# Attention and feed-forward in one kernel: a cosine with one sine, four pooled score products per late pair, and another way of setting the order of instructions

## The chip, the cores and the metric

The kernel runs on one core of a Trainium2 chip. The metric is the device time of one execution in microseconds. The engines are TensorE (PE in the rows; PEld is its weight load), VectorE (DVE), ScalarE (ACT), GpSimd (POOL) and SyncE (SP), which issues most of the transfers. TensorE's clock has two levels, 1.2 and 2.4 GHz, and the rows give the granted clock as a share of full speed.

## What is computed

The reference, cut to what matters:

```python
batch, n_heads, seq, head_dim = (8, 8, 576, 64)
q_d = q.reshape(B, H, Sd, 4, D).mean(axis=3)      # k_d, v_d alike, Sd = 144
out_d = sm_attn(q_d, k_d, v_d)                    # softmax attention over 144 pooled positions
out_up = np.repeat(out_d, 4, axis=2)
mask = np.abs(pos[:, None] - pos[None, :]) < 4    # local attention of 7 neighbours
out_local = np.matmul(softmax(np.where(mask, scale * q @ k.T, -1e9)), v)
x = (out_up + out_local)                          # as (4608, 512)
h = x @ w_in                                      # (4608, 2048)
g = h * np.cos(h)
return g @ w_out                                  # (4608, 512)
```

All tensors are fp32 (the weights arrive as pairs of 32-bit words). The kernel makes up for 16-bit products by splitting each factor into a high and a low fp16 part.

## The kernel before, in words

**Work.** Two heads make a pair, so there are 8 x 4 = 32 pairs. A pair goes through five steps: `u_qk` loads q and k and pools them (sum over 4 positions), `u_v` loads v, `u_s` makes local and pooled scores and their softmax, `u_t` transposes the probabilities, `u_pv` multiplies by v and writes the result, as high and low part, into one of four tiles of x (384 tokens each, 12 of them in all). Batches 0 and 1 (`NEARLY` = 2) go through early forms of these steps, batch 1 in two parts (`part_s`, `part_t`, `part_pv`). The other six batches, 24 pairs, are the late pairs, whose scores are made in `late_s`: 48 local products and 16 pooled ones, the latter with 32 columns of weights each (line 912), both fp32, each shown as two instructions in the trace.

**Feed-forward.** For each of 12 token tiles and 16 chunks of 128 hidden features, `gemm1` (line 1410) makes h, `cosine` makes g = h cos(h) as high and low fp16, and `gemm2` (line 1430) adds to three output banks. From tile 4 on, `Quad` (line 1335) makes h of two chunks by a scheme with fewer products. There are 192 calls of `cosine`, each on 128 x 384 values. It works by lines 1386 to 1393: ACT adds a large constant so that the sum rounds to whole turns, DVE subtracts it and h, ACT takes the sine of half the angle and the square, DVE makes h (sin^2 - 1/2), ACT rounds to fp16 (gh), POOL or DVE takes the rest (gl, line 530).

**Weights.** `w_load` and `w_split` bring and split each weight chunk (lines 575 to 590), `sum_w`, `sum_x` prepare sums for `Quad`, and `square`, `range_w` and `judge` watch that the 16-bit form is allowed.

**Order.** Nothing is issued in the order of the code. Each operation is entered into a `Plan` with its engine (or a choice of engines), a duration, what it reads and writes, the mean use that TensorE makes of its time (`util`) and its number of TensorE instructions (`num`). `run` places operations by a key, engine by engine, `schedule` improves the keys by running forwards and backwards, then tries the changes in `PICKS` (random additions to keys in a window of time) and keeps each that shortens the planned time. `run` holds a model of stops for TensorE's instructions (`FETCH`). The figures that the planner has for a pair of batch 0 are: local scores 1.30 us at a share of 0.25, pooled scores 0.65 at 0.42, two transposing products of 0.29 at 0.31, pooled values 2.10 at 0.51, local values 1.52 at 0.16.

**Unread products.** TensorE's clock falls when it has little to do. When the order stands, the code at the end walks through it and puts products of an identity that nobody reads (`wide`, line 1600, 128x512) into idle stretches of TensorE, spread behind the operations that it waits for, and more of them where its share over a trailing stretch would fall below `share` = 0.42 (`again` = 0.72 for a while after a planned stop), for operations planned before `watch` = 115 us.

**Stores.** `gemm2` copies each finished bank (line 1448) and SP stores it (line 1454); the last three copies end the program.

## Time and profile before

| | |
|---|---|
| runs | 914.15, 909.73, 913.79 us; median 913.79 |
| profiled execution | span 910.3 us from first to last instruction; no other time is given for it |
| TensorE busy | 889.4 us (98%), mean granted clock 0.994 |
| DVE, ACT, POOL busy | 711.2, 693.1, 486.2 us |
| instructions | 28740 |
| moved by DMA | 103.96 MB |

Busy TensorE includes the unread products. Products overlap in the pipeline, so a group of them is read from its start to the start of the next group, as the chain of waits does, and not from the mean duration. The chain is the work that ended last, followed back from the last instruction. Idle time of an engine other than the one that bounds a stage costs nothing.

### The profile page before, as it was taken

How to read it: one execution, taken by the hardware profiler on the slowest of the kernel's cores; microseconds unless marked ns; L12 is line 12 of the kernel's file. 1: busy time of each engine (PE TensorE's matmuls, PEld its weight loads, DVE VectorE, ACT ScalarE, POOL GpSimd, SP SyncE). 2: the span in 40 equal slices, each digit the busy share in tenths (PEclk: the TensorE clock that was granted, in tenths of full speed). 3: DMA queues.
4: the chain of work that ended last, by engine and by line, in shares of the span. 5: the costliest groups of instructions: out<-in, count | busy, mean ns of one | idle time of the engine just before them, and what ended most of it. 6: DMA issues, size and time to landing. Idle time of an engine off the chain costs nothing.

```text
span 910.3 us, 28740 instructions
## 1 busy us (share of the span) xinstructions
PE 889.4 (98%) x11673; PEld 579.9 (64%) x11673; DVE 711.2 (78%) x1514; ACT 693.1 (76%) x1542; POOL 486.2 (53%) x601
## 2 busy tenths in 40 slices
PE   8999999999999999999999999999999999999996
PEld 4665665555555555677767677666776777777773
DVE  6479788888889998877689887986689867846772
ACT  3458898888678876886887886986888987776764
POOL 4288753537768875644356543653468734522221
PEclk9899999999999999999999999999999999999998
DMA  7864176205453743232433443344344431124501
GB/s 245 255 223 142 37 276 214 83 1 95 113 131 80 169 99 99 63 94 67 119 88 101 121 114 96 89 111 125 102 135 119 112 105 38 56 96 140 174 2 39
DMA packets 100863, 103.96 MB, mean 114 GB/s; under 512 B 47280, under 2 KB 73648, under 8 KB 100720
## 3 DMA queue, kind: packets, MB, share of 16 engines
q1 hardware_dynamic: 99424, 99.67, 37.5%
q0 software_dynamic: 1296, 2.36, 1.8%
q8 instruction: 93, 1.52, 0.7%
q14 instruction: 50, 0.41, 0.1%
HBM read 81.05 MB, written 16.22 MB: 107 GB/s over the span
## 4 chain that ended last, share of the span: by engine, by line
PE 83%; DVE 7%; ACT 5%; DMA 2%; issue 2%; POOL 1%; SPq 0%; DVEq 0%; POOLq 0%; ACTq 0%
PE bank L1430 36%; PE bank L1335 22%; PE bank L1410 11%; PE bank L1600 3%; PE bank L906 2%; PE bank L1203 1%; PE bank L1184 1%; PE bank L912 1%; DMA q<-qT 1%; PE bank L1179 1%; DVE prob L932 1%; PE bank L1196 1%; PE bank L858 1%; ACT L946 1%; ACT L1389 1%
## 5 line engine op out<-in xcount | busy, mean ns | idle before, releaser
L1335 PEld LDWEIGHTS <-wdi 128*128 128x128 f16 x2400 | 203.8, 98 | 59.7 <-issue 3.8
L1430 PE MATMUL bank<-wdo,gh 128*128 128x512 f16 x696 | 207.1, 379 | 0.0
L1335 PE MATMUL bank<-wdo,wdi 128*128 128x192 f16 x1344 | 141.7, 246 | 0.8 <-DVE wdi L1356 0.3
L1430 PE MATMUL bank<-wdo,gl 128*128 128x512 f16 x348 | 131.7, 379 | 0.0
L1410 PEld LDWEIGHTS <-wdi 128*128 128x128 f16 x768 | 74.3, 98 | 56.3 <-issue 2.4
L530 POOL TENSOR_TENSOR gl<-tr,gh 128x384 f16<-128x384 f32 x60 | 59.2, 987 | 69.3 <-ACT gh L1393 51.0
L1430 PEld LDWEIGHTS <-gh 128*128 128x128 f16 x696 | 63.9, 98 | 41.4 <-issue 1.5
L1430 PE MATMUL bank<-wdo,wdi 128*128 128x512 f16 x342 | 86.9, 379 | 0.5 <-ACT ob L1448 0.5
L1430 PE MATMUL bank<-wdo,wdo 128*128 128x512 f16 x315 | 79.8, 379 | 0.7 <-ACT ob L1448 0.7
L1389 ACT ACTIVATE tr<-tr 128x384 f32<-128x384 f32 x98 | 50.9, 521 | 20.8 <-DVE tr L1387 20.3
L1430 PEld LDWEIGHTS <-gl 128*128 128x128 f16 x348 | 34.0, 98 | 41.1
L1386 ACT ACTIVATE tr<-bank,bmagic 128x384 f32<-128x384 f32 x66 | 37.8, 573 | 19.0 <-PE bank L1410 9.9
L1390 ACT ACTIVATE tr<-tr 128x384 f32<-128x384 f32 x98 | 50.4, 517 | 1.2
L1391 DVE SCALAR_TENSOR_TENSOR tr<-tr,bank 128x384 f32<-128x384 f32 x66 | 36.0, 545 | 18.0 <-ACT tr L1390 17.7
L1430 PEld LDWEIGHTS <-wdo 128*128 128x128 f16 x342 | 32.1, 98 | 28.1 <-issue 1.7
L1430 PEld LDWEIGHTS <-wdi 128*128 128x128 f16 x342 | 32.2, 98 | 27.2 <-issue 1.5
L530 POOL TENSOR_TENSOR gl<-wdo,gh 128x384 f16<-128x384 f32 x28 | 26.2, 937 | 43.3 <-ACT gh L1393 31.5
L1251 DVE TENSOR_TENSOR rec<-rec 128x192 f32<-128x192 f32 (+2 forms) x92 | 47.0, 512 | 0.7
L1351 DVE TENSOR_TENSOR bank<-bank,wdo 128x384 f32<-128x384 f32 x64 | 35.9, 560 | 14.6 <-PE bank L1335 13.8
L956 POOL TENSOR_TENSOR prob<-prob,su 128x432 f32<-128x432 f32 x24 | 24.4, 1018 | 37.9 <-DVE su L953 28.7
L530 POOL TENSOR_TENSOR wdo<-rec,wdo 128x384 f16<-128x384 f32 (+1 forms) x36 | 34.1, 953 | 17.2 <-ACT wdo L1296 11.2
L530 POOL TENSOR_TENSOR gl<-wdi,gh 128x384 f16<-128x384 f32 x28 | 28.3, 1010 | 26.6 <-ACT gh L1393 25.6
(408 smaller groups left out, 2451.8 us busy)
## 6 DMA issues: line engine op xcount, KB each, us to landing
vl<-vl SPq DMA_DIRECT2D x26, 384.0 KB, 3.8
vd<-vdn SPq DMA_DIRECT2D x24, 384.0 KB, 3.9
wdi<-w_in SPq DMA_DIRECT2D x16, 512.0 KB, 6.0
wdo<-w_out SPq DMA_DIRECT2D x16, 512.0 KB, 7.4
again<-w_in SPq DMA_DIRECT2D x32, 256.0 KB, 3.4
again<-w_out SPq DMA_DIRECT2D x32, 256.0 KB, 3.6
q<-qT SPq DMA_DIRECT2D x26, 292.0 KB, 4.0
k<-kT SPq DMA_DIRECT2D x26, 292.0 KB, 3.9
```

The lines of the kernel that those rows point to most:

```text
L530: f = lambda e: lambda: e.tensor_tensor(out=out(), in0=in0(), in1=in1(), op=ALU.subtract)
L956: f = lambda e, get=get, by=by: lambda: e.tensor_tensor(out=get(), in0=get(), in1=by(), op=ALU.mult)
L1251: f = lambda e: lambda: e.tensor_tensor(out=out(), in0=in0(), in1=in1(), op=op)
L1335: pe.matmul(bank.get()[:, half * HT:(half + 1) * HT], w(i, a), x(l, a), start=start and k == 0, stop=k == 5, skip_group_check=not start)
L1351: pl.op("DVE", _dve(TT), lambda: dve.tensor_tensor(out=by.get()[:, :TT], in0=by.get()[:, :TT], in1=s.get(), op=ALU.add), r=[mid, s], w=[by])
L1386: pl.op("ACT", _act(m, banked, 1), lambda: act.activation(tr.get(), h(), AF.Identity, bias=bmagic), r=r, w=[tr])
L1389: pl.op("ACT", _act(m, False), lambda: act.activation(tr.get(), tr.get(), AF.Sin, scale=PI / fm.h), w=[tr], tab="sin")
L1390: pl.op("ACT", _act(m, False), lambda: act.activation(tr.get(), tr.get(), AF.Square, scale=math.sqrt(fm.ratio)), w=[tr])
L1391: pl.op("DVE", _dve(m), lambda: dve.scalar_tensor_tensor(out=tr.get(), in0=tr.get(), scalar=0.5 * fm.ratio, in1=h(), op0=ALU.subtract, op1 ...
L1410: pe.matmul(ph.get()[:, :m], w[:, i, kc, :], x[:, kc, :], start=(n == 0), stop=(n == 3 * KC - 1))
L1430: pe.matmul(o, (gh, gh, gl)[k].get()[:, sl], wo.get()[:, (0, 1, 0)[k]], start=(c == c0 and k == 0), stop=(c == c1 - 1 and k == 2))
L1600: return pe.matmul(s[2].get(), ident_b, ident_b.unsqueeze(1).broadcast_to([P, 4, P]), start=True, stop=True)
```

## The change

Three parts.

**Cosine.** ACT divides h by a turn, adds a quarter and writes int32, so that the conversion rounds to whole turns; DVE multiplies the turns back and subtracts h; ACT takes one sine with a quarter turn as bias, which is the cosine; DVE multiplies by h. The square is gone.

**Pooled scores of late pairs.** Four products with 128 columns of weights take the place of 16 with 32. The sixteen columns of queries that are left over are now read at other partitions, so a subtraction and two small stores use other row groups.

**Order and unread products.** `FETCH` goes from `run`. A new `replay` walks through each planned order, with stops for instructions in blocks of 256, and sets the unread products while it walks; the search takes its total as the score. The share is 0.60 everywhere before 140 us. `PICKS` is a longer list, all of whose entries are applied one after the other, to keys or to the choice of engine. Durations and counts of the planner are adapted. A weight split can be staged in PSUM where `SPLIT` says so, which returns 0. One of the last three stores is issued by ACT.

```diff
-FETCH = (448, 10.6, 256, 17.0, 5.2, 3.6)
+BLOCK, FIRSTS, SEQ, FETCH, CROWD, WARM = 256, 448, 105, 3.8, 1.0, 4.6
...
-CFG = dict(cold=6.8, queue=0.0, alttol=0.9, iters=8, mix=0.0, tabpen=3.2, lat=0.2, latself=0.13, latpe=0.25, late=0.17, port=1.0, lead=5.0, lead0=14,
-           fgap=0.4, f0=0.8, fend=300.0, warm=0, fill=0.8, share=0.42, again=0.72, cool=6.0, watch=115.0)
+CFG = dict(cold=6.8, queue=0.0, alttol=0.9, iters=8, mix=0.0, tabpen=3.2, lat=0.2, latself=0.13, latpe=0.25, late=0.17, port=0.55, lead=5.0, lead0=14,
+           fgap=0.4, f0=0.8, fend=300.0, warm=0, fill=0.85, share=0.6, again=0.72, cool=6.0, watch=140.0)
...
             total, start = self.run(key, False)
-            if best is None or total < best[0]:
-                best = (total, start, key)
+            score = self.replay(start)
+            if best is None or score < best[0]:
+                best = (score, start, key)
...
+        for kind, seed, lo, width, sigma, share in self.picks:
             for o in self.ops:
-                if lo <= best[1][o][0] < lo + width and rnd.random() < share:
-                    key[o] += rnd.gauss(0, sigma)
+                if lo <= best[1][o][0] < lo + width and draw(seed, o.i, 0) < share:
+                    x = sigma * (draw(seed, o.i, 1) + draw(seed, o.i, 2) + draw(seed, o.i, 3) - 1.5)
+                    if kind:
+                        self.lean[o] = self.lean.get(o, 0.0) + x
+                    else:
+                        key[o] += x
...
+    def replay(self, start):
...
+        def burst(t, dur, n, ready):
+            nonlocal used, edge, limit, seq
+            step, left, first = dur / max(1, n), n, used
+            seq = max(seq, ready)
+            if edge < first + n:
+                x = max(seq + (edge - first) * 0.0045, when(edge - SEQ))
+                asked.append(x + FETCH + (CROWD if x > 60.0 and any(a + 1.5 < x < b for a, b in full[-3:]) else 0.0))
+                edge += BLOCK
+            while left:
+                k = min(left, limit - used)
+                if not k:
+                    t, limit = max(t, asked.pop(0)), limit + BLOCK
+                    seq = max(seq, t)
+                    continue
+                t, used, left = t + k * step, used + k, left - k
...
+                    for (x, d), (y, _) in zip(marks, marks[1:] + [(t - 0.2, None)]):
+                        j, stop = 0, x + (y - x) * CFG["fill"]
+                        while max(free["PE"], x) + 0.22 < stop:
+                            wide(x)
+                            j += 1
...
+                    if 4.0 < o.start < CFG["watch"]:
+                        j = 0
+                        while j < 16:
+...
                            wide(0.0)
+                            j += 1
...
+    SPLIT = lambda k, c: 0
...
             for i in range(2):
-                for g in range(4):
-                    for h in range(2):
-                        hs, at = slice(64 * h, 64 * h + 64), SD - BS if i else BS * g
-                        pe.matmul(banks[h].get()[BS * g:BS * (g + 1), i * SD:(i + 1) * SD], qkd.get()[hs, 0, at:at + BS], qkd.get()[hs, 1, :],
-                                  start=True, stop=True)
-        pl.op("PE", 1.55, mm, r=[q, k, qkd], pw=banks, w=loc + poo, slack=SLACK, num=256)
+                for h in range(2):
+                    hs = slice(64 * h, 64 * h + 64)
+                    at = (SD - P + BS * h) * i
+                    few = qkd.get()[hs].rearrange("p a n -> p (a n)")[:, at:at + P]
+                    pe.matmul(banks[h].get()[:, i * SD:(i + 1) * SD], few, qkd.get()[hs, 1, :], start=True, stop=True)
+        pl.op("PE", 1.55, mm, r=[q, k, qkd], pw=banks, w=loc + poo, slack=SLACK, num=209)
...
-        less(1, lambda: smd.get()[BS:2 * BS, 2:3, :SD], slice(1, 2), [wide0], BS, 2 * BS)
+        less(1, lambda: smd.get()[2 * BS:3 * BS, 2:3, :SD], slice(1, 2), [wide0], 2 * BS, 3 * BS)
...
-        pl.op("ACT", _act(m, banked, 1), lambda: act.activation(tr.get(), h(), AF.Identity, bias=bmagic), r=r, w=[tr])
-        pl.op("DVE", _dve(m), lambda: dve.scalar_tensor_tensor(out=tr.get(), in0=tr.get(), scalar=MAGIC * fm.h, in1=h(),
-                                                               op0=ALU.subtract, op1=ALU.subtract), r=r, w=[tr], shares=not banked)
-        pl.op("ACT", _act(m, False), lambda: act.activation(tr.get(), tr.get(), AF.Sin, scale=PI / fm.h), w=[tr], tab="sin")
-        pl.op("ACT", _act(m, False), lambda: act.activation(tr.get(), tr.get(), AF.Square, scale=math.sqrt(fm.ratio)), w=[tr])
-        pl.op("DVE", _dve(m), lambda: dve.scalar_tensor_tensor(out=tr.get(), in0=tr.get(), scalar=0.5 * fm.ratio, in1=h(),
-                                                               op0=ALU.subtract, op1=ALU.mult), r=r, w=[tr], shares=not banked)
+        turns = lambda: tr.get().bitcast(I32)
+        pl.op("ACT", _act(m, banked), lambda: act.activation(turns(), h(), AF.Copy, scale=1.0 / fm.h, bias=0.25), r=r, w=[tr])
+        pl.op("DVE", _dve(m), lambda: dve.scalar_tensor_tensor(out=tr.get(), in0=turns(), scalar=fm.h, in1=h(),
+                                                               op0=ALU.mult, op1=ALU.subtract), r=r, w=[tr], shares=not banked)
+        pl.op("ACT", _act(m, False, 1), lambda: act.activation(tr.get(), tr.get(), AF.Sin, scale=-2.0 * PI / fm.h, bias=quarter), w=[tr], tab="sin")
+        pl.op("DVE", _dve(m), lambda: dve.scalar_tensor_tensor(out=tr.get(), in0=tr.get(), scalar=-0.5 * fm.ratio, in1=h(),
+                                                               op0=ALU.mult, op1=ALU.mult), r=r, w=[tr], shares=not banked)
...
+                    if end and i == 2:
+                        pl.op("ACT", 0.4, lambda dst=dst, ob=ob: act.dma_start(dst, ob.get()), r=[ob], w=[part[(t, i)]], lat=2.0)
+                    else:
+                        dma(2048 * P, lambda dst=dst, ob=ob: sp.dma_start(dst, ob.get()), r=[ob], w=[part[(t, i)]])
```

## Rows read from the trace of the kernel before

**Rows 1.** The page, first section: span, and busy time, share and instructions by engine.

```profile
span 910.3 us, 28740 instructions
PE 889.4 (98%) x11673; PEld 579.9 (64%) x11673; DVE 711.2 (78%) x1514; ACT 693.1 (76%) x1542; POOL 486.2 (53%) x601
```

**Rows 2.** Busy time by stretch: length, busy us and count by engine; clock, DMA, GB/s.

```profile
25.00:30.00 5.00, 5.00 (x33) 3.29 (x29) 2.69 (x6) 1.06 (x2) 0.67 (x1) 0.51 0.77 231
30.00:35.00 5.00, 5.00 (x92) 2.58 (x92) 0.00 (x0) 0.00 (x0) 0.00 (x0) 0.81 0.82 271
...
35.00:57.00 22.00, 22.00 (x564) 17.16 (x558) 14.12 (x33) 11.31 (x37) 14.18 (x22) 1.00 0.64 193
57.00:93.00 36.00, 35.05 (x428) 18.73 (x426) 31.37 (x70) 29.85 (x68) 31.50 (x40) 1.00 0.59 188
93.00:901.80 808.80, 801.03 (x10091) 525.98 (x10090) 647.06 (x1363) 640.01 (x1401) 429.78 (x501) 1.00 0.37 103
```

**Rows 3.** The unread products (L1600) alone: length, PE and PEld busy, clock, DMA.

```profile
7.20:57.00 49.80, 18.46 (x64) 6.25 (x64) 0.93 0.73 227
57.00:93.00 36.00, 12.87 (x51) 4.41 (x51) 1.00 0.59 188
```

**Rows 4.** The chain that ended last, start-up: start us, us, what.

```profile
10.95 1.19 issue
...
14.66 0.69 PE bank L1037 x8
...
22.51 1.61 issue
...
24.51 3.50 PE bank L1179 x32
28.01 5.91 PE bank L1600 x18
33.93 1.52 PE bank L1196 x96
...
41.01 2.11 PE bank L1179 x32
...
99.36 0.42 PE bank L768 x4
```

**Rows 5.** ACT by line and shape (busy us, mean ns); last, L1389 in a stretch.

```profile
L1386 ACT ACTIVATE tr<-bank,bmagic 128x384 f32<-128x384 f32 x66 | 37.8, 573 | 19.0 <-PE bank L1410 9.9 <-DVE bank L1351 8.3 <-POOL x2l L530 0.3
L1386 ACT ACTIVATE tr<-wdi,bmagic 128x384 f32<-128x384 f32 x11 | 6.7, 610 | 0.4
L1389 ACT ACTIVATE tr<-tr 128x384 f32<-128x384 f32 x98 | 50.9, 521 | 20.8 <-DVE tr L1387 20.3
L1316 ACT ACTIVATE wdo<-bank 128x192 f32<-128x192 f32 x64 | 20.7, 323 | 4.6 <-PE bank L1335 4.4
L1448 ACT ACTIVATE ob<-bank 128x512 f32<-128x512 f32 x21 | 12.4, 594 | 3.9 <-PE bank L1430 3.2 <-POOL gl L530 0.5 <-POOL wdo L530 0.2
L575 ACT ACTIVATE xxh<-wdi,bhalf 128x512 int32<-128x512 uint32 x16 | 12.2, 759 | 1.7 <-POOL wdo L589 1.7
...
57.00:93.00 36.00, 5.93 (x7) 1.00 0.59 188
```

**Rows 6.** TensorE in order of time, end of one late pair's scores.

```profile
256.33 0.76 PE L912 MATMUL bank<-qkd 64*32 64x144 f32 x30
257.02 2.12 PE L1430 MATMUL bank<-wdo,wdi 128*128 128x512 f16 x9
```

**Rows 7.** What TensorE waited for after 93 us: us, times, longest.

```profile
PE bank L1335 <- DVE wdi L1391: 1.3, 1, 1.3
PE bank L1430 <- ACT ob L1448: 1.3, 2, 0.7
PE bank L1410 <- DVE tr L1391: 1.0, 1, 1.0
```

**Rows 8.** The chain that ended last, its end.

```profile
894.20 7.57 PE bank L1430 x35
```

More of the change, by code (lines that the diff above doesn't have):

```diff
@@ L239, in run @@
         locked = False
-        cur, pen, tol, queue = None, CFG["tabpen"], CFG["alttol"], CFG["queue"]
-        issued, edge, there = CFG["lead0"], FETCH[0], FETCH[1]
+        cur, pen, tol, lean = None, CFG["tabpen"], CFG["alttol"], {} if back else self.lean
         start, n = {}, 0
@@ L362, in _mmr, with before @@
+    def before(self, o, t):
+        seen, out, todo = set(), [], [o]
+        while todo:
+            for d, _ in todo.pop().preds:
+                if id(d) not in seen and d.end > t:
+                    seen.add(id(d))
+                    todo.append(d)
+                    if d.eng in ("ACT", "DVE", "POOL"):
+                        out.append(d)
+        return sorted(out, key=lambda d: (d.end, d.i))
 def _mmr(n, k, small):
```

258 lines of the change are left out of this document (142 added, 116 removed), and 47 rows, old and new, of the table PICKS.

## The prediction

> **What bounds the kernel now.** I read the page's first two sections, then the busy time by stretch, the chain that ended last in order of time, the costliest groups by line and shape, and TensorE's waits. TensorE is busy for 889.4 of 910.3 us [rows 1]. From 93.0 us to the last product at 901.8 us it works 801.0 of 808.8 us, at full clock, while ACT is busy 640.0 us, DVE 647.1 and POOL 429.8 [rows 2]. There nothing can be gained but TensorE work itself and the 7.8 us in which it stood still. Before 93 us it is busy too, but part of that is the products that nobody reads (L1600): 18.46 us between 7.2 and 57 us, 12.87 us between 57 and 93 [rows 3]. So the start-up is the only stage with much to win.
>
> One stretch stands out. Between 25 and 30 us the granted clock is 0.51, between 30 and 35 us 0.81, and in the latter five DVE, ACT and POOL do nothing at all [rows 2]: they wait for TensorE. The chain shows what TensorE does there: a stop of 1.61 us at 22.51 that no wait explains, the first L1179 group in 3.50 us where a later one takes 2.11, then 18 unread products in 5.91 us, then L1196 [rows 4]. No other engine works towards the operands of L1196 in the last five of these microseconds, so the 18 products themselves stood on the path. The clock fell to the lower of its two levels (1.2 GHz) after the stop at 22.51.
>
> **The change, part by part.**
>
> *Cosine.* Per cosine (192 of 128x384) ACT now does an add of the rounding constant, 0.573 us from PSUM or 0.61 from SBUF, a sine of 0.521 and a square, about 0.52 like the sine; DVE does two scalar_tensor_tensor. After it ACT copies to int32 and takes one sine with a bias tile; DVE keeps two. A copy from PSUM takes 0.323 us for 192 columns and 0.594 for 512, so by interpolation 0.323 + 192/320 x 0.271 = 0.486 for 384. The bias tile costs 0.61 - 0.52 = 0.09, so the sine becomes 0.61. That is 1.10 instead of 1.61 us, 0.52 less per cosine, 99 us of ACT's 693 [rows 1, 5]. Writing int32 is not seen in this form; L575 writes 512 of them in 0.759 us with a bias tile and a strided source, against 0.594 for the copy of 512, so it adds between nothing and (0.759 - 0.594) x 384/512 = 0.12 us; I take nothing, since the 0.09 of the bias explains most of it. DVE's two are of the same kind and size as before: zero. Between 93 and 901.8 us this ACT time lies beside TensorE, which is the cover. What can come out is the waits that end with a cosine's DVE step or an ACT instruction: 1.3 + 1.0 after L1391 and 1.3 after L1448, together 3.6 us [rows 7]. Another order also makes waits; I take 1.8 us off, between 3.6 off and 1.0 on. Between 57 and 93 us all three helpers are near full (DVE 31.4 us of 36, POOL 31.5, ACT 29.9 [rows 2]) and about four cosines run (5.93 us in seven entries of the sine's line, loads of its table among them [rows 5]); they shorten ACT by 4 x 0.52 = 2.1 us, which is the most, nothing is the least, and I take 1.5.
>
> *Pooled score products.* In each of the 24 late pairs 16 products with 32 columns of weights (32 instructions in the trace, fp32 in two passes) become 4 with 128 (8 instructions). The 32 run from 256.33 to the next group at 257.02, 0.69 us [rows 6]. The nearest rows for 8 are L1037 with 72 columns of weights, 0.69 us [rows 4], while L768, 4 instructions with 96 columns, holds the chain for 0.42 us [rows 4]. Twice L768 is an upper end of 0.84; once, if the four overlap entirely, a lower one of 0.42: per pair +0.15 to -0.27 us, in all +3.6 to -6.5. L1037 is nearest, with the same 8 instructions on the same 144 columns, and its 0.69 says that the columns streamed four times are what costs, and those stay; for the wider weights I add 0.05: +1.2 us in all, on TensorE and so on the path. By the Trainium skill (page "TensorEngine Tiling (Array Packing)", section "Tiling Modes") a change of tiling mode drains TensorE; the 16 keep the split that the local products before them use, the four do not, so by that rule each pair pays a drain more and the sum would lie between 1.2 and 3.6 instead of at 1.2. The planner keeps 1.55 us for the operation and sees neither. The moved row groups in the subtraction and in the two small stores keep their sizes: zero.
>
> *Staging in PSUM.* SPLIT returns 0 for every chunk, so the new branch of the weight split is never taken: zero.
>
> *Last store from ACT's queue.* The copies and stores follow the last products, which end at 894.20 + 7.57 = 901.77 us [rows 8], and SP has nothing else then. One hop from ACT to SP goes, one issue comes to ACT, which has nothing behind it: zero. The same 7.57 us of products cover the last cosine's shorter chain: zero.
>
> *Order and unread products.* The planner now replays each order with the unread products and the instruction stops in it, and fills so that a trailing share of 0.60 (was 0.42, 0.72 after a predicted stop) is kept until 140 us (was 115). Four terms, before 57 us:
> - The 1.39 us that the first L1179 lost to the lower clock goes if the floor holds (0 to 1.4): 1.4.
> - The 5.91 us of unread products shrink to what the floor asks ahead of L1196. That group counts 0.16 of its 1.52 us, so to reach 0.60 about 1.8 us have to stand by it: 4.1 off, between 0 and 5.9.
> - The floor adds elsewhere. By the planner's own figures a pair of the first batch is 1.30 + 0.65 + 0.58 + 2.10 + 1.52 = 6.15 us of products that count 0.25, 0.42, 0.31, 0.51 and 0.16, 2.1 us in all; for 0.60 it needs (0.60 x 6.15 - 2.1)/0.40 = 4.0 us of filling, 16.0 for four pairs. Present now, without the 5.91, are 18.46 - 5.91 = 12.55; with the 1.8 it is 14.35. So 1.65 more, of which I put half where TensorE waits anyway: 0.8 on, between 0 and 16.0 - 12.55 = 3.5.
> - The stops of 1.19 us at 10.95 and 1.61 at 22.51 end without a wait on another engine [rows 4]. The replay plans around such stops; whether it can is open, 0 to 2.8, and I take half: 1.4 off. The Trainium skill holds that fetching instructions is hidden behind issue (page "Runtime: NRT & Kernel Launch", section "Instruction fetch mechanics"); by it there would be no such stop to plan around and this term would be 0. The two rows with an idle TensorE speak against it here.
>
> Together 1.4 + 4.1 - 0.8 + 1.4 = 6.1 us off at 57 us. Between 57 and 93 us DVE, ACT and POOL are each 83 to 88% busy, so not all of it arrives; I carry 0.8 of it, 4.9.
>
> **Sum.** 910.3 - 4.9 - 1.5 - 1.8 + 1.2 = 903.3 us against the profiled span, the only time that the page gives for that execution. The runs shown go from 909.73 to 914.15 with a median of 913.79, so the profile is one of the quick ones and their median lies 3.5 us above it. A floor should make the early clock steadier; I keep half of that distance, 1.8: 905.1, rounded to **905.0 us**.
>
> **The rivals.**
> - *Given back before 93 us.* DVE (31.4 of 36 us) and POOL (31.5) are the bound of that stage, and what starts earlier waits there. Then 4.9 becomes 1 and 1.5 becomes 0.5: 910.3 - 1.0 - 0.5 - 1.8 + 1.2 + 1.8 = 910. For it: those shares; against it: 12.87 us of unread products in the stage show that TensorE is not what it waits for, but also that order can matter. Chance 0.22.
> - *The search finds more.* The 12.87 us between 57 and 93 us are time in which TensorE had nothing; an order that fills two thirds of the 36 us better takes 8 us more: 897. For it: ACT is 0.52 us shorter per cosine just where ACT is on the chain; against it: the other two engines. Chance 0.13.
> - *The floor is the new bound (slower).* Between 35 and 57 us TensorE works 22.00 of 22 us already [rows 2]. If the extra filling stands on the path, the third term is 3.5 on instead of 0.8. The groups of the second batch, worked out in the same way from the planner's figures, ask up to 20 us by themselves, where 12.87 stand now: 7.1 on. The late pairs cost their 3.6, and only the 4.1 and the 1.8 come off: 913.8 + 3.5 + 7.1 + 3.6 - 4.1 - 1.8 = 922. It decides from the point where the unread products between 7.2 and 93 us sum to more than now (31.3 us [rows 3]) with the chain running through them. Against it: between the second batch's groups stand feed-forward products that count in full. Chance 0.11.
> - Forecast: 0.54.
>
> A measurement of this kernel can tell about 0.5% from no change: 909.2 and 918.4 are the bounds. Faster: nine tenths of the forecast, all of the second, a third of the first rival: 0.49 + 0.13 + 0.05 = 0.67, taken as 0.66. Slower 0.11, same 0.23. The range reaches from the second rival, with 2 us for its size, to beyond the first, 895 to 915; the floor's case is left out above, a little of the search's below.
>
> **What would show it.** Right: no stretch below full clock after the first 10 us, the group before L1196 in under 2.5 us, L1390's square gone and ACT near 594 us, the late pooled group at 0.65 to 0.85 us. Wrong: L1600 above 31.3 us between 7.2 and 93 us, most of it in the chain, the steady rate first reached at 93 us or later, or new waits over 4 us after 93 us. I would be wrong by most if the ACT time were worth something between 93 and 900 us, as TensorE has only 7.8 idle us there.

## The result, and the profile after

The changed kernel takes **926.0 us** in the median of four runs (922.86 to 926.5), the kernel before 912.9 beside it. The ratio is 1.0149, with an interval of 1.0113 to 1.0184: slower by 1.5%, where 905 us and "faster" had been forecast, outside the range. The profiled execution has a span of 924.1 us, 13.8 more than that of before. Its own time is 925.94 us: a time lies 1.8 us above the span of the same execution, here and in every run below, so spans are compared with spans.

The page's first section of the changed kernel, against [rows 1]:

```profile
span 924.1 us, 27475 instructions
PE 899.4 (97%) x11128; PEld 587.9 (64%) x11128; DVE 721.6 (78%) x1543; ACT 605.8 (66%) x1323; POOL 498.4 (54%) x616
```

ACT has lost 87.3 us, and the end has not come earlier. TensorE has 10.0 us more work and 3.8 us more without work. Next the busy time of the changed kernel by stretch (length, busy us and count for PE, PEld, DVE, ACT, POOL, then clock, DMA share, GB/s), against [rows 2]:

```profile
25.00:30.00 5.00, 5.00 (x135) 3.87 (x136) 1.21 (x3) 0.69 (x2) 0.00 (x0) 1.00 0.92 294
30.00:35.00 5.00, 5.00 (x128) 3.42 (x127) 3.74 (x11) 2.03 (x6) 2.34 (x4) 1.00 0.77 239
35.00:57.00 22.00, 22.00 (x431) 14.52 (x431) 10.63 (x25) 8.96 (x31) 11.23 (x17) 1.00 0.67 193
57.00:93.00 36.00, 34.49 (x518) 19.17 (x512) 29.09 (x69) 25.58 (x58) 27.49 (x35) 1.00 0.41 141
```

The clock no longer falls, as foreseen. But in the 22 us from 35 to 57 the helpers work less than before (DVE 10.63 us in place of 14.12, POOL 11.23 in place of 14.18) while TensorE is never free. The unread products alone (L1724 now, L1600 in [rows 3]), and below them the first feed-forward group of the kernel before and of the changed one (count, ns, first and last start):

```profile
7.20:57.00 49.80, 25.66 (x103) 8.88 (x103) 1.00 0.77 228
57.00:93.00 36.00, 13.21 (x50) 3.90 (x50) 1.00 0.41 141
```

```profile
L1410 PE MATMUL bank<-x0h,wdi x48: 322/326/337, 59.9 to 96.3; 128*128 128x384 f16 x48
L1561 PE MATMUL bank<-x0h,wdi x48: 322/326/337, 63.6 to 99.0; 128*128 128x384 f16 x48
```

They sum to 38.87 us, 7.5 more than before, and the first feed-forward product starts at 63.6 us, where the kernel before has 59.9. What stands in the way is seen in the chain of the changed kernel (start us, us, what), against [rows 4]:

```profile
8.24 1.62 PE bank L1724 x7
9.85 0.64 PE bank L1188 x8
...
11.73 0.76 issue
...
12.71 1.62 PE bank L1724 x7
14.32 0.64 PE bank L1188 x8
...
18.21 0.96 issue
...
23.16 1.83 PE bank L1724 x8
24.99 1.52 PE bank L1347 x96
26.51 1.19 PE bank L1724 x5
27.70 2.11 PE bank L1330 x32
29.81 0.97 PE bank L1724 x4
...
34.80 1.95 PE bank L1724 x9
36.74 1.52 PE bank L1347 x96
```

Read it downwards: most groups of attention have unread products right ahead of them, eight or nine ahead of each L1347 and five ahead of each L1330, and the chain passes through them. Of the 38.87 us, 26.7 are in the chain (before: 18.0 of 31.3). L1347 (L1196 before) starts for the first time at 24.99, not at 33.93, so the start was much better at that point; when it starts for the third time, at 45.73 against 45.17, the lead is gone.

### The profile page after: what moved, and what is told of

Same layout as the page of the kernel before. It is cut to its first block, busy times and chain, and to the rows that moved or that the text cites. A ratio compares the mean times of both kernels' runs of the same rounds, so it can differ in the third digit from the quotient of the medians.

```text
span 924.1 us, 27475 instructions
## 1 busy us (share of the span) xinstructions
PE 899.4 (97%) x11128; PEld 587.9 (64%) x11128; DVE 721.6 (78%) x1543; ACT 605.8 (66%) x1323; POOL 498.4 (54%) x616
## 4 chain that ended last, share of the span: by engine, by line
PE 70%; DVE 13%; POOL 7%; ACT 3%; issue 3%; DMA 2%; SPq 1%; DVEq 0%; POOLq 0%; ACTq 0%
PE bank L1581 29%; PE bank L1486 21%; PE bank L1561 5%; PE bank L1724 4%; DVE rec L1402 2%; PE bank L1057 2%; PE bank L1354 2%; DMA k<-kT 2%; PE bank L1335 1%; PE bank L1064 1%; POOL qkd L822 1%; PE bank L1330 1%; DVE tr L1539 1%; DVE xxh L728 1%; DVE qkd L827 1%
## 5 line engine op out<-in xcount | busy, mean ns | idle before, releaser
L1561 PEld LDWEIGHTS <-wdi 128*128 128x128 f16 x768 | 74.3, 98 | 57.6 <-issue 2.9
L677 POOL TENSOR_TENSOR gl<-tr,gh 128x384 f16<-128x384 f32 x56 | 57.2, 1023 | 68.7 <-ACT gh L1544 35.6
L1581 PEld LDWEIGHTS <-gh 128*128 128x128 f16 x696 | 63.6, 98 | 40.1 <-issue 0.2
L1541 ACT ACTIVATE tr<-tr,quarter 128x384 f32<-128x384 f32 x98 | 60.0, 613 | 38.3 <-DVE tr L1539 37.9
L1542 DVE SCALAR_TENSOR_TENSOR tr<-tr,bank 128x384 f32<-128x384 f32 x66 | 36.0, 546 | 13.3 <-ACT tr L1541 13.1
L1724 PE MATMUL bank<-ident_b 128*128 128x512 bf16 x166 | 44.6, 400 | 1.6 <-POOL ident_b masks.py:199 1.3
L1538 ACT ACTIVATE tr<-bank 128x384 int32<-128x384 f32 x66 | 31.8, 482 | 21.7 <-DVE bank L1502 15.8
L1541 ACT ACTIVATE wdo<-wdo,quarter 128x384 f32<-128x384 f32 x47 | 28.9, 614 | 20.9 <-DVE wdo L1539 20.8
L1539 DVE SCALAR_TENSOR_TENSOR tr<-tr,bank 128x384 f32<-128x384 int32 x66 | 35.8, 542 | 8.0 <-ACT tr L1538 7.6
```

The costliest lines, as they stand in the source:

```text
L677: f = lambda e: lambda: e.tensor_tensor(out=out(), in0=in0(), in1=in1(), op=ALU.subtract)
L1538: pl.op("ACT", _act(m, banked), lambda: act.activation(turns(), h(), AF.Copy, scale=1.0 / fm.h, bias=0.25), r=r, w=[tr])
L1539: pl.op("DVE", _dve(m), lambda: dve.scalar_tensor_tensor(out=tr.get(), in0=turns(), scalar=fm.h, in1=h(), op0=ALU.mult, op1=ALU.subtract), ...
L1541: pl.op("ACT", _act(m, False, 1), lambda: act.activation(tr.get(), tr.get(), AF.Sin, scale=-2.0 * PI / fm.h, bias=quarter), w=[tr], tab="sin")
L1542: pl.op("DVE", _dve(m), lambda: dve.scalar_tensor_tensor(out=tr.get(), in0=tr.get(), scalar=-0.5 * fm.ratio, in1=h(), op0=ALU.mult, op1=AL ...
L1561: pe.matmul(ph.get()[:, :m], w[:, i, kc, :], x[:, kc, :], start=(n == 0), stop=(n == 3 * KC - 1))
```

## The experiments

All ran in turn with the kernel before, whose median was 911.9 to 913.6 us in the four sets. Ratios are to it.

**1. The arithmetic alone, in the order of before.** In the kernel before, the cosine's and the pooled products' code is exchanged; the planner goes on counting the old steps, the square's step issues nothing, and so every engine keeps its order.

```diff
-    act.activation(tr, h, AF.Identity, bias=bmagic)
+    act.activation(turns, h, AF.Copy, scale=1.0 / fm.h, bias=0.25)
...
-    act.activation(tr, tr, AF.Square, scale=math.sqrt(fm.ratio))
+    (nothing; the planner still counts 0.52 us)
```

> The kernel before with its order kept on every engine; in it the cosine is computed in the new way (int32 turns, one sine with a bias, no square) and the late pairs' pooled scores are four products. Planner, floor and unread products are those of before. Theory (the order and the floor cost the time, the two arithmetic edits cost nothing and are worth little): ACT falls by about 90 us to some 600, the time stays within 0.5% of before, ratio 0.995 to 1.000, 908 to 913 us. Rival 1 (the new arithmetic itself costs TensorE time): ratio 1.010 or more, 922 us or more. Rival 2 (the prediction's own: shorter cosines take waits off the path): 0.990 to 0.995.

Measured: 910.6 us, ratio 0.997 (0.9941 to 1.0); ACT fell from 693.1 to 613.5. Together the two edits do not cost, and with 80 us less of ACT they win at most 0.6%. In the profiled runs even the 3.6 us that it gained (906.7 against 910.3) were made in the start-up, where this execution kept its clock at 1.00 and began its feed-forward work at 56.2; from there to the end it took 850.5 us, the kernel before 850.4. In these 0.1 us are 3.1 that the pooled products cost (experiment 7), so by these two executions the cosine by itself takes off some 3.0, an estimate.

**2. The floor alone, in the order of the change.** One line ahead of the last replay; the order stays what it was.

```diff
+        CFG["share"], CFG["watch"] = 0.42, 115.0
         self.total = self.replay(best[1])
```

> The changed kernel in the same order on every engine, but the unread products are set with a floor of 0.42 until 115 us, as before, in place of 0.60 until 140. Theory (the floor's products stand on TensorE's path in the start-up): unread products before 93 us fall from about 43 us to 35 or less, the first feed-forward group starts 2 to 5 us earlier than at 63.6 us, the time falls by 3 to 6 us to 920 to 923 (ratio to before 1.007 to 1.011). Rival (the filling only fills waits that are there anyway): the first feed-forward group stays at 63 to 64 us, the time within 1 us of 926. Second rival (the clock falls in the start-up without the floor): granted clock under 0.9 somewhere between 10 and 60 us, and the time 926 or more.

Measured: **912.1 us**, ratio 1.0005 (0.9975 to 1.0035). In this order the floor costs 13.9 us, more than the 13.1 by which the change lost against before, and more than twice what I had expected of this run at most. Its unread products (first two rows) and its first feed-forward group:

```profile
7.20:57.00 49.80, 13.93 (x49) 3.87 (x49) 1.00 0.81 241
57.00:93.00 36.00, 5.13 (x19) 1.53 (x19) 0.95 0.54 171
```

```profile
L1562 PE MATMUL bank<-x0h,wdi x48: 326/326/524, 49.3 to 84.6; 128*128 128x384 f16 x48
```

19.8 us of unread products less, 14.3 us earlier at the first feed-forward group, 15.4 us earlier at the end of the span. The clock held without them (0.95 in the second row is a drop to 0.74 between 62 and 67 us, where TensorE waited). Counted by the group that they stand ahead of, the unread products of the changed kernel are 23.9 us ahead of batch 0 and 10.5 ahead of batch 1; here they are 8.7 and 6.6. Other levels followed, set in the same way (0.0, 0.30 and 0.50), and one run with two levels:

```diff
-    ... >= CFG["share"] * ...
+    ... >= (0.6 if o.start < 57.0 else 0.42) * ...
```

> The changed kernel in the same order, with no floor at all: unread products stand only where the replay sees TensorE idle. The run with the floor of 0.42 had 19.1 us of them between 7.2 and 93 us and 912.1 us, the changed kernel 38.9 us and 926.0. Theory (every unread product of the floor lies on the path and nothing else is in play): unread products near 13 us or less, the first feed-forward group at 45 to 48 us, 906 to 910 us. Rival (some floor is needed, because TensorE's granted clock falls without it): a granted clock under 0.9 in some stretch between 10 and 75 us, the first feed-forward group at 49 us or later, 912 us or more.

> The changed kernel in the same order with a floor of 0.30 until 115 us. Measured so far in this order: 919.5 us with no floor (granted clock 0.50 from 32 to 52 us), 912.1 with 0.42, 926.0 with 0.60. Theory (two prices, the unread products on the path above 0.42 and the fallen clock below it): the clock falls for part of the start-up and the time is 912 to 920 us. Rival (the clock holds with less too): granted clock 1.00 up to 57 us, the first feed-forward group at 47 to 49 us, 906 to 911 us.

> The changed kernel in the same order with a floor of 0.50 until 115 us. Theory (the price grows with the floor): unread products between 7.2 and 57 us between 13.9 and 25.7 us, the first feed-forward group between 49.3 and 63.6 us, 915 to 922 us. Rival (a step between 0.42 and 0.60, at the watch time or at the second batch): 912 or 926 us, within 1 us.

> The changed kernel in the same order, with the floor of 0.60 for operations planned before 57 us and of 0.42 from there to 115 us. Theory (the loss is made in the first batch, where attention alone gives TensorE work): unread products between 7.2 and 57 us as in the changed kernel, 25 us, between 57 and 93 us near 5 to 8; the first feed-forward group at 60 to 64 us, 920 to 926 us. Rival (the second batch's filling makes the loss, as the prediction's own rival has it with 7.1 of its 10.6 us): 913 to 917 us.

Measured: 919.5 us without a floor (ratio 1.0085), 910.4 with 0.30 (0.998, 0.9946 to 1.0015), 919.5 with 0.50 (1.0097), and 923.9 with 0.60 up to 57 us and 0.42 beyond (1.0136). Without a floor the rival was right, as the busy time by stretch of that run shows:

```profile
30.00:40.00 10.00, 9.53 (x148) 8.54 (x147) 5.66 (x10) 3.99 (x9) 6.48 (x10) 0.50 0.80 240
40.00:50.00 10.00, 10.00 (x181) 8.71 (x179) 4.57 (x11) 2.77 (x11) 5.95 (x8) 0.50 0.82 263
```

The granted clock is at its lower level (0.50 of full, 1.2 GHz) for these twenty microseconds, after a stretch, 22 to 27 us, in which TensorE was busy for 3.12 of 5 us. Even so its first feed-forward group starts at 55.3, eight microseconds ahead of the changed kernel with its full clock. (The profiled execution took 914.41 us; by the medians the lead over the changed kernel is 6.5 us.)

With 0.30 the clock of the profiled execution was 0.67 between 20 and 30 us and full from there to 57, and by the median this floor can't be told from 0.42. But its twelve executions fall into two groups: seven take 906.5 to 911.3 us at a mean granted clock of 0.989 to 0.997, five take 915.8 to 922.7 at 0.973 to 0.981. I read 0.30 as an edge, at which the clock holds in some executions only.

The run with 0.60 up to 57 us keeps 11.7 of the 13.9 us. It has 25.5 us of unread products ahead of batch 0 and 10.0 ahead of batch 1, so the loss is made in the first batch, as the theory had it. Two of its numbers I had wrong: its first feed-forward group starts at 65.3 us (60 to 64 expected) and between 57 and 93 us it has 12.48 us of unread products (5 to 8 expected). Its profiled execution took 929.13 us, 5.3 above the median.

**3. The same floor in the order of before.** Only the level, the watch time and a cap of 16 unread products ahead of an operation are changed.

```diff
-    share=0.42, again=0.72, cool=6.0, watch=115.0
+    share=0.6, again=0.72, cool=6.0, watch=140.0
...
-    while 4.0 < o.start < CFG["watch"] and share(...) < ...:
+    for j in range(16):
```

> The kernel before, nothing changed in it but the floor, 0.60 until 140 us in place of 0.42 until 115 (at most 16 unread products ahead of an operation, as in the changed kernel). Theory (the floor costs wherever it is set, through the attention groups of the start-up): unread products between 7.2 and 93 us 45 us or more in place of 31.3, the first feed-forward group 5 us or more later than at 59.9, ratio 1.008 to 1.02, 921 to 932 us. Rival (the floor is harmful only in the changed order): ratio 0.997 to 1.004.

Measured: 932.9 us, ratio 1.0238 (1.0209 to 1.0267), the theory's case and a little beyond: 45.3 us of unread products between 7.2 and 93 us, the first feed-forward group at 70.9. The floor harms in either order.

**4. Less filling in the order of before.** The higher floor after a predicted stop (`again`) from 0.72 to 0.42, and in another run both levels to 0.30, each on top of experiment 1.

```diff
-    share=0.42, again=0.72
+    share=0.42, again=0.42
+    share=0.30, again=0.30   (the other run)
```

> The kernel before in its own order with both arithmetic edits, as in the run at 910.6 us, and with one thing more: the higher floor of 0.72 that its planner asks after a predicted stop is 0.42 too. This tests the prediction's term of 4.1 us, the 18 unread products in 5.91 us ahead of one group. Theory (those products stood on the path): unread products between 25 and 57 us 3 us or more fewer than the 12.3 of that run, 904 to 908 us. Rival (they hold the clock after the stop, and it falls without them): granted clock under 0.85 between 25 and 57 us, 911 us or more.

> The order of before with both arithmetic edits, as in the run at 907.5 us, with a floor of 0.30 throughout in place of 0.42. Theory (what the floor asks above the clock's need lies on the path; in the changed order 0.30 and 0.42 came out alike, 910.4 and 912.1): 903 to 908 us, unread products between 7.2 and 57 us below 14.2. Rival (the clock falls in this order): granted clock under 0.9 between 10 and 57 us, 909 us or more.

Measured: **907.5 us**, ratio 0.9965 (0.9945 to 0.9985), and 914.0, ratio 1.0028 (0.9999 to 1.0058). The first is faster than both kernels, by 0.35% than before and by 2% than the change; from experiment 1 (0.997) it can't be told apart by the time, though its profile has what was foreseen. Unread products of the run at 907.5, then one line of experiment 1's chain, and the chain of the run at 907.5 where [rows 4] had the 5.91 us:

```profile
7.20:57.00 49.80, 14.22 (x52) 4.11 (x49) 1.00 0.83 245
57.00:93.00 36.00, 10.87 (x44) 3.90 (x44) 1.00 0.51 164
```

```profile
26.32 3.99 PE bank L1602 x18
```

```profile
22.05 0.64 PE bank L1179 x6
22.69 0.26 issue
22.95 1.88 PE bank L1179 x26
24.82 0.75 PE bank L1602 x3
25.58 1.52 PE bank L1196 x96
```

Three unread products in 0.75 us stand where eighteen stood, and L1196 starts at 25.58, 8.35 us earlier than before. Not all of that is theirs: in experiment 1, whose clock held, the eighteen took 3.99 us and L1196 started at 30.32. So they are worth 3.2 us at full clock, and 1.9 of the 5.91 us before were the lower clock. At 0.30 the same order loses its clock (run at 914.0, by stretch):

```profile
27.00:30.00 3.00, 2.40 (x75) 2.06 (x78) 2.27 (x8) 1.64 (x6) 1.92 (x4) 0.90 0.93 326
30.00:57.00 27.00, 27.00 (x405) 22.86 (x400) 11.70 (x26) 8.48 (x29) 12.85 (x20) 0.50 0.71 208
```

27 us at the lower level, and that with 7.3 us of unread products left before 57 us; the changed order, with 9.1, had 0.83 between 10 and 20 us, 0.67 between 20 and 30, and its full clock behind in the profiled execution. I had expected this run to win or tie: a miss.

**5. ACT's work put back.** One more square of 128x384 per cosine, into a tile that nobody reads, in the changed kernel (floor 0.60 and 0.42) and in the kernel before.

```diff
+        act.activation(junk[:, :m], tr, AF.Square)
```

> The changed kernel in its own order, with one ACT square of 128x384 more per cosine between the sine and the multiply, into a tile that nobody reads: the ACT load and the length of the cosine's chain are again those of before, about 100 us more ACT. Theory (TensorE bounds, and ACT's relief is hidden): 926 to 929 us, ratio to before 1.014 to 1.018. Rival (the relief is worth time in this order and something else eats more): 932 us or more, ratio 1.021 or more.

> The run at 912.1 us (changed order, floor 0.42) with one ACT square per cosine more, read by nobody: what ACT's relief is worth in this order when the start-up isn't held up by the floor. Theory (the order leans on ACT's relief whatever the floor, as under 0.60 where it was worth 31 us): 935 to 945 us. Rival (with the floor gone from the path other engines have slack early, and the relief matters less): 912 to 925 us.

> The kernel before with one ACT square more per cosine, into a tile that nobody reads, in the order of before: about 100 us more ACT, 76% to 87%. The changed kernel lost 31 us by the same addition, while the order of before won only 3 us by the square's removal. Theory (an order is fitted to its costs: taking work from an engine that is not the bound gives little, adding as much breaks the fit): ratio 1.02 to 1.04, 931 to 949 us. Rival (only the changed order leans on ACT): ratio under 1.01.

Measured: 957.4 us (1.0489), 947.5 (1.0403) and 947.8 (1.04), that is 31, 35 and 36 us more than the same kernels without it (the last against 911.9). The theory of the first run, that TensorE bounds and ACT is hidden, fell; the second came out above its 935 to 945 us, the third as its theory had it. Of some 91 us of added ACT (page of the third run: 784.3 us) more than a third comes out there, 36. Yet experiment 1 took 80 us away from the same order and won some 3.0 us behind the start-up. TensorE's waits (engine, line, waited for; us, times, longest) in the kernel before with two squares, against [rows 7]:

```profile
PE bank L1411 <- DVE tr L1392: 6.0, 3, 4.4
PE bank L1335 <- DVE tr L1392: 4.5, 8, 0.9
PE bank L1431 <- ACT ob L1449: 3.7, 4, 1.6
PE bank L1335 <- DVE wdi L1392: 3.3, 4, 1.8
```

The waits behind the cosine's DVE step and the copies of L1449 have grown from 4.0 us (the 3.6 of [rows 7] and 0.4 more of L1335) to 17.5 in these four rows, mostly in small pieces, and TensorE's idle time between 93 and 880 us from 7.8 to 31.3. I read it so: the order had hidden the cosine just to its length, no further, so that work taken away finds little to free and work added is seen at once. The square adds to ACT's load and to the length of each cosine; which of the two counts wasn't separated.

**6. New orders.** The kernel before replanned by its own planner with both edits; the changed kernel searched under 0.42; the changed kernel without its draws, filled at 0.42.

```diff
+    the cosine and the pooled products of the change, with its costs   (in the kernel before)
...
-    share=0.6, again=0.72, cool=6.0, watch=140.0                       (second run)
+    share=0.42, again=0.72, cool=6.0, watch=115.0
...
-    pl.picks = PICKS if small else ()                                  (third run, with the line of experiment 2)
+    pl.picks = ()
```

> The kernel before with the new cosine and the four pooled products, planned anew by the old planner with the shorter costs (floor 0.42 until 115 us, constant port 1.0, the old draws, which were made for another order). Theory: no slower than before, 905 to 914 us, ratio 0.991 to 1.002; unread products between 7.2 and 93 us near 31 us. Rival 1 (the arithmetic costs): 922 us or more. Rival 3 (any new order without draws made for it loses several us): 915 to 922 us.

> The changed kernel, its whole search run with the floor of 0.42 until 115 us, so that the order too is chosen under it (the draws were made under 0.60 and may not suit). Theory (the floor alone is at fault): 908 to 914 us, like the run with the order kept. Rival (an order for which no draws were made loses, as the replanned kernel of before did with 927.8): 918 us or more, with more idle TensorE after 93 us.

> The changed kernel without the list of draws (the order is the planner's own best by replay, under a floor of 0.60), and with unread products set by a floor of 0.42 until 115 us. Theory (an order without its draws loses some 15 us, as the two replanned kernels at 927.5 and 927.8 did): 920 to 932 us, with more idle TensorE after 93 us than the 16 us of the run at 912.1. Rival (the draws are worth little and those two lost by something else): 910 to 916 us.

Measured: 927.8 us (1.0178), 927.5 (1.0172), 923.3 (1.0121). All three lose, the second as its rival had it and the third as its theory. The first lies where rival 1 had it (the arithmetic costs), which experiment 1 excludes, and above rival 3's 915 to 922: a new order loses, and more than I had given it. They lose in different places. The first takes 866.1 us from its first feed-forward group (60.3) to the end, where the order of before takes 850.4. The second begins its feed-forward work early, at 54.5, but has 24.9 us of idle TensorE between 93 and 880 us (before: 7.8). In the third the clock is 0.51 from 40 to 65 us, that work starts at 64.6, and from there to the end it takes 864.1 us, 4.7 more than the run at 912.1; it idles 16.7 us between 93 and 880 (the run at 912.1: 10.5). So its 11 us can't all be put down to the missing draws. The profiled executions of the second and the third took 932.38 and 930.57 us, 4.9 and 7.3 above their medians, and the other six of the third had a mean granted clock of 0.988 to 0.994, not 0.98: how much of the 11 us the clock is stays open.

**7. The pooled products undone**, in the run at 912.1 us: sixteen of 32 columns again, with the row groups that belong to them.

```diff
-    few = qkd[hs].rearrange("p a n -> p (a n)")[:, at:at + P]
-    pe.matmul(banks[h][:, i * SD:(i + 1) * SD], few, qkd[hs, 1, :])
+    for g in range(4): pe.matmul(banks[h][BS * g:BS * (g + 1), i * SD:(i + 1) * SD], qkd[hs, 0, at:at + BS], qkd[hs, 1, :])
```

> The run at 912.1 us (changed kernel, same order, floor 0.42) with the late pairs' sixteen products of 32 columns of weights back in place of four of 128. Theory (144 columns streamed four times either way, 0.69 us per pair in both traces): 911 to 914 us, within 0.3% of it. Rival 1 (the prediction's +0.05 per pair, or more, is real): 907 to 911 us. Rival 2 (the four are quicker): 914 to 919 us.

Measured: 914.6 us, ratio 1.0031 (1.0001 to 1.0061) against 1.0005 (0.9975 to 1.0035). By the number that is rival 2's case (the four are quicker), just above the theory's, but the intervals overlap: the times don't settle it. The traces do, if the whole score step is read and not the pooled group alone. In the kernel before the first pooled products start while the last local ones still run, so the 0.69 us from 256.33 on in [rows 6] are not all of their time. The step of a late pair, of which [rows 6] has the end, starts with this row in the kernel before:

```profile
255.50 0.99 PE L906 MATMUL bank<-k,q 64*32 64x32 f32 x94
```

In the changed kernel a whole step, with the next group, is:

```profile
273.59 1.02 PE L1057 MATMUL bank<-k,q 64*32 64x32 f32 x96
274.54 0.76 PE L1064 MATMUL bank<-qkd 64*128 64x144 f32 x8
275.24 1.47 PE L1581 MATMUL bank<-wdo,wdo 128*128 128x512 f16 x6
```

From the first local product to the next group (257.02 before) it is 1.52 us before and 1.65 in the changed kernel. The median over the late pairs is 1.52 in each of the four profiles with sixteen products, this run's among them, and 1.65 in each of the fourteen with four. So the four cost 0.13 us per pair, 3.1 us in all. Rival 1 was right in its mechanism, and the executions scatter too much to show it.

**The start-up and the end, side by side.** Start of the first feed-forward group, span, and what lies between, in the profiled executions:

| kernel | first feed-forward | span | between |
|---|---|---|---|
| before | 59.9 | 910.3 | 850.4 |
| arithmetic alone, order of before | 56.2 | 906.7 | 850.5 |
| the same, `again` 0.42 | 52.4 | 902.5 | 850.1 |
| the same, 0.30 | 61.7 | 909.8 | 848.1 |
| before, floor 0.60 | 70.9 | 928.4 | 857.5 |
| changed | 63.6 | 924.1 | 860.5 |
| changed, 0.60 to 57 us | 65.3 | 927.3 | 862.0 |
| changed, 0.50 | 56.6 | 917.1 | 860.5 |
| changed, 0.42 | 49.3 | 908.7 | 859.4 |
| changed, 0.30 | 48.8 | 909.5 | 860.7 |
| changed, no floor | 55.3 | 912.5 | 857.2 |
| changed, 0.42, pooled products undone | 52.7 | 914.5 | 861.8 |
| changed, square back | 61.5 | 953.4 | 891.9 |
| changed, 0.42, square back | 52.3 | 944.8 | 892.5 |
| before, two squares | 57.6 | 946.5 | 888.9 |
| before replanned | 60.3 | 926.4 | 866.1 |
| changed, searched under 0.42 | 54.5 | 930.5 | 876.0 |
| changed, no draws, 0.42 | 64.6 | 928.7 | 864.1 |

Within the order of before and that of the change, without the square, the last column stays within 848.1 to 850.5 and 857.2 to 862.0, apart from the floor of 0.60 in the order of before, which also fills beyond 93 us: what the filling does to the first group it does to the end, nearly one for one. Between the two orders it differs by 10 us. That is the second half of the result: the changed order, freed of its floor, starts its feed-forward work 10.6 us earlier than before and gives 9.0 of them back.

Where it gives back is shown, and what bounds it there; why the planner chose so is not. From the first feed-forward group to the last product, TensorE idles 14.3 us in the changed kernel (852.0 less 837.7 busy) and 8.7 before (841.9 less 833.2), and most of the difference lies between 93 and 200 us. Experiment 1 has the arithmetic of the change in the order of before: 6.7 us of idle TensorE there (842.0 less 835.3). So the order alone adds 7.6 us of idle time, and 2.4 of busy time that are not unread products (10.1 us of them, 11.1 in experiment 1) and stay open. The busy time from 93 to 200 us, of the changed kernel and then of the kernel before:

```profile
93.00:200.00 107.00, 102.00 (x1131) 57.74 (x1130) 98.22 (x169) 83.12 (x170) 91.21 (x107) 1.00 0.43 146
```

```profile
93.00:200.00 107.00, 106.20 (x1180) 60.02 (x1179) 90.29 (x167) 92.86 (x193) 58.17 (x68) 1.00 0.38 130
```

DVE and POOL are up from 90 and 58 us to 98 and 91, ACT is down: the new order has drawn work forward that these two do (23.6 us of it on POOL are the additions of L1402, which has 1.6 us there in the order of before), and TensorE idles 5 us instead of 0.8. Of these, 1.9 and 0.6 us end with ACT, 1.0 with DVE and 1.3 is a stop without a wait; none ends with POOL. But the chain does pass through the helpers. In the kernel before, 101 of these 107 us of the chain are TensorE's. In the changed kernel 21 are, with 36 on POOL, 19 on DVE and 16 on ACT; in the run at 912.1 us 7, with 23, 39 and 20. So TensorE, busy as it is, no longer sets the pace there, and an earlier start of its feed-forward work waits for the helpers. Whether the lowered `port` cost, the draws or the score by replay chose so wasn't tried by itself; the order without draws was no better (864.1).

## Why the prediction was wrong, point by point

**Where the 21 us are.** The span was to be 903.3 us and is 924.1. The first feed-forward group was to start some 4.9 us earlier and starts 3.7 later, which makes 8.6 of the 20.8 us; from there to the end 2.1 us were to come off and 10.1 came on, which makes 12.2. Experiment 1 puts 0.1 of the 10.1 on the two edits, so the rest is the order's. So two steps failed, the floor's term and the order behind 93 us. The 1.8 us that I added for the scatter of the executions came out right by luck: a time lies 1.8 us above the span of its own execution, and that is what the sum lacked.

**The stage was right, the sign of the step was wrong.** That the start-up can win, and that the 18 unread products stood on the path, held: with three in their place (experiment 4) L1196 starts 4.7 us earlier than in experiment 1, and in the changed kernel eight in 1.83 us stand there, as the second term had it. But the step "the floor adds elsewhere: 0.8 on, between 0 and 3.5" failed. The unread products before 57 us are 25.66 us, not 16.0, and those in the chain before 57 us went from 14.7 to 23.8, 9.1 more. The second and third terms together were to take 3.3 off. Two things were wrong in that term. I took half of the addition for waiting time, and the chain before 57 us has nothing in it but products and the two stops. And I averaged the share over a whole pair, while `replay` asks it ahead of each operation for the short stretch that ends with it: what was filled ahead of L1347 no longer counts a group later, so L1330 has five more ahead of it (1.19 us), and the transposing products behind that four again (0.97).

**The other two terms of the start.** The first (1.4 from the lower clock) came in: L1330 takes 2.11 us where [rows 4] has 3.50. The stops were to give 1.4: they are 0.76 and 0.96 in place of 1.19 and 1.61, 1.1 off. So both were right and were outrun. What I overlooked of the stops is where they come. Counted in products and weight loads, they come after 444 and 952 instructions of TensorE in the kernel before and after 444 and 696 in the changed one. The other profiles have them before 50 us after 444, 696, 950 to 952, 1202 to 1204, 1458, 1968 or 2218 and nowhere else: 444 and multiples of 252 to 254 more, whatever the order and the filling. So a place in the instruction stream sets them, not an operand; the planner's blocks of 256 instructions assume as much. The Trainium skill's page "Runtime: NRT & Kernel Launch", section "Instruction fetch mechanics", has fetching hidden behind issue; these stops, of 0.2 to 2.2 us with TensorE idle and no other engine waited for, speak against it, though no trace here shows the fetch itself.

**The rival had the mechanism.** "The floor is the new bound" gave 922 us, at a chance of 0.11; 926.0 was measured, and its condition, more than 31.3 us of unread products with the chain through them, is met (38.87, with 26.7 in the chain). Its sum was off in the place: it put 7.1 us on the second batch, where the unread products hardly rose (13.21 against 12.87), and 3.5 on the first, which makes 11.7 of the 13.9. Its 3.6 for the late pairs came close (3.1). What I set against it, that feed-forward products stand between the groups, holds for the second batch alone.

**Cosine.** The prices were right: the copy to int32 takes 0.482 us (0.486 worked out), the sine with its bias 0.613 (0.61), and writing int32 adds nothing. The cosine's lines on ACT fell from 311.5 us to 212.6, the 99 us worked out; ACT's busy time as a whole fell by 87.3 only, and I haven't followed the rest. ACT, by line and shape in the changed kernel, against [rows 5]:

```profile
L1541 ACT ACTIVATE tr<-tr,quarter 128x384 f32<-128x384 f32 x98 | 60.0, 613 | 38.3 <-DVE tr L1539 37.9
L1538 ACT ACTIVATE tr<-bank 128x384 int32<-128x384 f32 x66 | 31.8, 482 | 21.7 <-DVE bank L1502 15.8 <-PE bank L1561 3.5 <-POOL wdo L677 2.2
```

The worth was right as far as it can be told: 1.5 and 1.8 were carried, 3.3 in all, and experiment 1, with the 3.1 of the pooled products taken out, leaves some 3.0. What failed altogether is the step that left the order out of the sum behind 93 us. "Another order also makes waits" had an upper end of 1.0; TensorE's idle time behind the first feed-forward group rose by 5.6. Its longest waits in the changed kernel after 93 us, and one for a cosine, against [rows 7]:

```profile
PE bank L1581 <- ACT ob L1599: 3.1, 2, 1.9
PE bank L1486 <- DVE wdo L1497: 2.0, 2, 1.7
PE bank L1057 <- DVE vd L1366: 1.4, 1, 1.4
PE bank L1561 <- DVE tr L1542: 1.0, 1, 1.0
```

The waits for the cosine's last DVE step are still there (1.7 us with another row of 0.7, before 2.7), and those for the copies of L1599 have grown (4.3 us with another row of 1.2, before 1.3), although ACT has 87 us less to do. [rows 7] leave out the longest wait of before, 1.6 us of L1335 for POOL's L530.

**Pooled products.** +1.2 was carried for 0.05 per pair; it is 0.13 per pair, 3.1 in all, near the upper bound of 3.6. The rows were read from the start of the pooled group on, which leaves out what stands ahead of it: the first of the sixteen products starts 0.80 us after the first local one (256.30 against 255.50), the first of the four 0.95 (274.54 against 273.59). By the Trainium skill's page "TensorEngine Tiling (Array Packing)", section "Tiling Modes", a change of tiling mode drains TensorE, and the trace agrees: the 0.13 us stand where the split changes from 64x32 to 64x128.

**The last store** cost nothing, as said: the chain of the changed kernel ends with the same 7.57 us of products as [rows 8].

```profile
908.34 7.57 PE bank L1581 x35
```

**The chances.** The forecast and the two faster cases shared one premise, that the floor's products mostly fill waits; the row against it, TensorE at 22.00 of 22 us between 35 and 57 [rows 2], had been read and was given to a rival of 0.11. The first rival, in which DVE and POOL take back an earlier start, was put before 93 us at 0.22; the chain shows it behind 93.

## What to carry to other kernels

Filling that keeps a clock up is work on the engine that bounds: price each filler by whether the chain passes through it, and where an engine is busy for all of a stretch, price all of it as path. Set its level by trying several in the same order, since too little and too much both lost 7 to 14 us here, and 0.30, in one order level with 0.42 by the median, lost the clock for 27 us in the other. Look at every execution, too: a level at the edge shows as two groups of times. And a kernel with a searched order can't be costed by taking durations off its old trace: keep the order and change the arithmetic alone, then change the order alone. A group of products is priced together with the one ahead of it: read from its own start, the pooled group hid its cost.

## What the runs showed of the hardware that was not expected

- A conversion to int32 on ACT's way out cost nothing: 482 ns from PSUM for 384 columns, which the copies of 192 and 512 columns (323 and 594 ns) put at 486.
- Behind 96 fp32 instructions with 64x32 weights, 8 instructions with 64x128 weights take longer than 32 with 64x32, both streaming 144 columns: 1.65 us for the whole step in place of 1.52, although either group takes 0.69 us from its own start.
- With its clock at the lower level for some twenty microseconds of attention, the run without a floor still reached its feed-forward work 8 us before the changed kernel at full clock (55.3 against 63.6): the fallen clock was cheaper than 20.7 us of filling.
- TensorE's stops without a wait in the first 50 us come after 444 products and weight loads and then at multiples of 252 to 254 more, in all the profiles that have any (seventeen of eighteen), with their different orders and fillings. They last 0.2 to 2.2 us, and not every such place has one.
